# Chunk attention and FNet mixing: the token transform on even and odd tokens apart, in four 32-row parts

## The chip, the cores and the metric

The kernel runs on one core of one Trainium2 chip, in float32. Its time is the device time of one execution in microseconds. Nothing but the kernel's own launch is counted.

## The reference

```python
# q, k, v: [B=8, H=8, S=576, D=64]; attention inside chunks of 64 tokens
scores = (q_c @ k_c.T) / sqrt(D); attn = softmax(scores); x = attn @ v_c
x = x.transpose(0, 2, 1, 3).reshape(8, 576, 512)
mixed = real(fft(fft(x, axis=1), axis=2))     # over tokens, then over the 512 features
u = x + mixed
un = (u - mean(u)) / sqrt(var(u) + 1e-6)      # over the features
out = u + relu(un @ w_ch1[512, 2048]) @ w_ch2[2048, 512]
```

Two Fourier transforms of real data have symmetries. The sum of a row and its mirror image carries the cosine part, the difference the sine part, in tokens as in features, so that products of half the size do.

## The kernel before

**Tiles.** The 9 chunks of a batch are laid out as tiles of 128 rows: two LO tiles (chunks 2i and 2i+1), two HI tiles (the mirrored chunks from the end, 8-2i and 7-2i), and chunk 4, which two batches share as one tile of rests. For the mirroring the first token of each low chunk must stand one chunk further on: `shift(b)` (L477) moves six rows of 512 around, from tile to tile; it does so with six small DMAs, on GpSimd's queue for b = 1 and on SP's from b = 2. `shift_early` (L464) does the same for b = 0 with copies.

**Stages of a batch.** `attention(b)` computes a tile's transposes (L333), scores (`sc`, L384), softmax, and products with v (`att_V`, L432 to L460). `fold(b, i)` (L491) adds and subtracts a LO and a HI tile and their feature mirrors into `pm`: four quarters T = 0 to 3 of 128 columns, and one middle column; `i = NM = 2` is the tile of rests. GpSimd does this for b >= 2, VectorE for b = 1. `fourier(b)` (L644) is the token transform and then the feature transform. `product` (L652) multiplies the quarters of `pm` with the table `tk` of 289 = S/2 + 1 cosines or sines: eight matmuls of 128 rows x 289, four of 64 rows x 289 for the rests, and twelve one-column products for the middle columns, in four pieces of 73 or 70 each. ScalarE copies the results from PSUM into `zf` and `zr` (L678 to L688). `mixed(i)` (L700) multiplies them with the feature tables; `both` (L710, L711), `added` (L717) and `means` (L637 to L642) build u and the layer norm. Batch 0 has its own `fourier_early` (L745 and on).

**MLP.** The tiles go through the MLP in nine groups of 512 tokens: group g = 0 to 7 holds the LO and HI tiles of batch g, group 8 the four tiles of rests. Groups 0 and 1 use the weights as loaded, which VectorE and ScalarE round first (L285 to L322). For later groups seven products take the place of eight (`up_halves` with L1040, `down_halves` with L1089); their combined weights are computed while groups 0 and 1 run (`keep1`, `keep2`, stored to DRAM at L902 and L920) and fetched by SP as slabs (L926 to L932). A full MLP step is 16 passes of 128 x 256, 3.45 us of TensorE. GpSimd's largest share is L941, sums of pieces of `h` in which the MLP's products go on.

**Order.** Each engine runs its queue in program order. The main loop steps through `mlp(g)`; between two steps it advances the generator `side(b)` of the next batch as often as is needed to end at a given step (`ready_at`; the number of yields of a side stands in `sizes`). A side is `attention(b)`, then PAUSE = 3 empty steps, then `fourier(b)`. A step that returns true is "heavy": the rounding of the next weight piece is skipped beside it. Around Fourier in batch 2 the order on TensorE is: last product with v, 17.3 us of MLP, four token products, 3.5 us, the other twenty, 3.5 us, the first feature product. In odd batches from 3 it is 19.0 us of MLP, four products, 1.7, twenty, 6.9, feature products; in even ones from 4 it is 17.3, four, 3.5, twenty, 3.5.

**DMA.** SP issues nearly all transfers: q, k (L195), v (L218), the slabs and the stores. `store` (L871) writes a LO tile with one DMA, a HI tile with two, a tile of rests with four (of the last, half on ScalarE's queue). DMAs issued by SP and ScalarE take eight completion semaphores in turn, in program order over both, and a DMA waits with its issue for the one that had its semaphore before.

**Start.** `load_tables` (L224) loads the token tables with 8 DMAs; `turn_tables` (L248) turns them with five ScalarE copies into `tk` before batch 0's first products.

Of the kernel before, what the change touches and what calls it, by code (L numbers as in the profile page):

```python
# [8 lines left out]
FP32 = mybir.dt.float32  # L9
# [7 lines left out]
def kernel(  # L17
# [67 lines left out]
    tk = const.tile([128, NM + 1, 2, NQ], FP32, name="tk")  # L85
# [3 lines left out]
    so = const.tile([128, HQ], FP32, name="so")  # L89
    wa = const.tile([128, KD * DFF], FP32, name="wa")  # L90
# [71 lines left out]
    pms, sts = {}, {}  # L162
    start = one_p.tile([128, KF * 512], FP32, tag="big", name="start")
# [5 lines left out]
    v_ring = [const.tile([128, 2, NJ, DV], FP32, name=f"v{i}") for i in range(3)]  # L169
    more_v = one_p.tile([128, 4 * NL + 64], FP32, tag="zf", name="more_v")  # L170
# [4 lines left out]
    def load(n, which="qk"):  # L175
# [4 lines left out]
        for src, dst, nm, eng in ((q, qs, "q", nc.sync), (k, ks, "k", nc.scalar if n == 0 else nc.sync)):  # L180
            if nm not in which:
                continue
            if n < first[1]:
                i = 2 * n + (nm == "k")
                t = start[:, (4 + i) * DM:(5 + i) * DM].rearrange("p (j r d) -> p j (r d)", r=2, d=D)
            else:
                t = one_p.tile([128, NJ, 4 * D], FP32, tag=nm, name=nm)
# [36 lines left out]
    def load_tables():  # L224

        t = start[:, 0:(NM + 1) * 2 * NQ].rearrange("p (i r f) -> p i r f", i=NM + 1, r=2)
        for c in range(2 * NM):  # L230
            (i, r0), (j, p0) = divmod(c * CH, 128), divmod((NC - 1 - c) * CH, 128)
            nc.sync.dma_start(out=t[r0:r0 + CH, i], in_=seq_tab[p0:p0 + CH, j])
        for r0 in (0, CH):
            nc.sync.dma_start(out=t[r0:r0 + 1, NM], in_=seq_tab[0:1, 0])
            nc.sync.dma_start(out=t[r0 + 1:r0 + CH, NM], in_=seq_tab[1:CH, NM])
        for i in range(2):
            nc.sync.dma_start(out=first_rest[32 + 32 * i:33 + 32 * i, 0:DM], in_=dim_tab[0:1, 1 + 2 * i, :])
# [9 lines left out]

    def turn_tables():  # L248
        t = start[:, 0:(NM + 1) * 2 * NQ]
        a, b = tk.rearrange("p i r f -> p (i r) f"), t.rearrange("p (i f) -> p i f", f=NQ)  # L250
        for c in range(2 * NM):
            nc.scalar.copy(a[:, :, c * CH:(c + 1) * CH], b[:, :, (c + 1) * CH:c * CH:-1])
        nc.scalar.copy(a[:, :, NL:NL + 1], b[:, :, 0:1])
        nc.scalar.copy(a[:, :, NL + 1:NQ], b[:, :, NL + 1:NQ])
# [157 lines left out]
    def att_P(n):  # L412
        ex = es.pop(n)
        pt = turn(lambda j: ex[:, j].rearrange("p e k -> p (e k)"))
        t = one_p.tile([128, NJ, 128], FP32, tag="pT", name="pT")
        nc.scalar.copy(t, pt)
        pT[n] = t
# [45 lines left out]

    def shift_early(i):  # L464

        lows = [xt(at[LO, 0, j])[:, 0:DM] for j in range(NM)]
        rest, kept = xt(rests[0])[0:1, 0:DM], first_rest[0:1, 0:DM]
        if i == 0:
            nc.gpsimd.tensor_copy(kept, lows[1][0:1])
            nc.gpsimd.tensor_copy(lows[1][0:1], lows[1][CH:CH + 1])  # L470
            nc.gpsimd.tensor_copy(lows[1][CH:CH + 1], rest)
        else:
            nc.scalar.copy(rest, lows[0][0:1])
            nc.scalar.copy(lows[0][0:1], lows[0][CH:CH + 1])
            nc.scalar.copy(lows[0][CH:CH + 1], kept)

    def shift(b):  # L477

        lows = [xt(at[LO, b, i]) for i in range(NM)]
        r = b % 2 * CH  # L480
        rest = xt(rests[b // 2])[r:r + 1, 0:DM]
        eng = nc.gpsimd if b < 2 else nc.sync
        t = three_p.tile([128, XW], FP32, tag="y", name="first")
        for i in range(NM):
            eng.dma_start(out=t[2 * i:2 * i + 2, 0:DM], in_=lows[i][0:CH + 1:CH, 0:DM])
        eng.dma_start(out=t[2 * NM:2 * NM + 1, 0:DM], in_=rest)
        for i in range(NM):
            eng.dma_start(out=lows[i][0:CH + 1:CH, 0:DM], in_=t[2 * i + 1:2 * i + 3, 0:DM])
        eng.dma_start(out=rest, in_=t[0:1, 0:DM])

    def fold(b, i):  # L491
# [7 lines left out]
        if i < NM:  # L499
            pm = two_p.tile([128, DM + 1], FP32, tag="pm", name="pm")  # L500
# [5 lines left out]
        else:  # L506
            pm = two_p.tile([128, 2 * HQ + 1], FP32, tag="pm_rest", name="pm_rest")
# [10 lines left out]
        if i < NM:  # L518
# [3 lines left out]
            to = pm[:, 3 * HQ:DM + 1:HQ]  # L522
        else:
            for T, op in enumerate((ALU.add, ALU.subtract, ALU.subtract, ALU.add)):
                to = pm[T % 2 * CH:T % 2 * CH + CH, T // 2 * HQ:T // 2 * HQ + HQ]
                eng.tensor_tensor(out=to, in0=near[:, T // 2], in1=far[:, T // 2], op=op)
            to = pm[CH:, HQ:2 * HQ + 1:HQ]
        eng.tensor_copy(to, two[p, HM + 1 + HQ:HQ - 1:-HM - 1])
        pms[b, i] = pm

    def attention_early():
# [33 lines left out]
        turn_tables()  # L565
# [64 lines left out]
    zr = const.tile([128, 4, 2, CH], FP32, name="zr")  # L630
# [12 lines left out]

    def fourier(b):  # L644
        h = b % 2
        zf = one_p.tile([128, 4 * NL + 64], FP32, tag="zf", name="zf")
        zf = zf[:, 0:4 * NL].rearrange("p (t f) -> p t f", t=4)
        pm = [pms.pop((b, i)) for i in range(NM + 1)]

        def product(T, i, out_, lhsT, start, stop, cols=slice(0, NQ)):  # L650
            p = slice(0, 128) if i < NM else slice(T % 2 * CH, T % 2 * CH + CH)
            nc.tensor.matmul(  # L652
                out=out_, lhsT=lhsT[p], rhs=tk[p, i, T // 2 if T != 5 else 0, cols],
                start=start, stop=stop, skip_group_check=True,
            )


        z = [ps_t.tile([128, 512], FP32, tag="pt", name="z") for _ in range(2)]
        more = ps_a.tile([128, 2, 512], FP32, tag="att", name="more_z")
        z += [more[:, k] for k in range(2)]  # L660
        for T in range(4):
            for i in range(NM):
                product(T, i, z[T][:, 0:NQ], pm[i][:, T * HQ:(T + 1) * HQ], i == 0, False)
            if T == 1:
                yield
        for T in range(4):
            product(T, NM, z[T][:, 0:NQ], pm[NM][:, T // 2 * HQ:(T // 2 + 1) * HQ], False, True)

        mids = []
        for g, c0 in enumerate(range(0, NQ, NS)):  # L670
            c1 = min(c0 + NS, NQ)
            mids.append((c0, c1, z[2][32 * g:32 * g + 1, NQ:NQ + c1 - c0]))
        for i in range(NM + 1):
            for c0, c1, out_ in mids:
                one = pm[i][:, DM:DM + 1] if i < NM else pm[i][:, 2 * HQ:2 * HQ + 1]
                product(5, i, out_, one, i == 0, i == NM, slice(c0, c1))
        for T in range(4):
            nc.scalar.copy(zf[:, T, :], z[T][:, 0:NL])  # L678
            nc.scalar.copy(zr[:, T, h, 0:NQ - NL], z[T][:, NL:NQ])
            upper, mirrored = zr[:, T, h, NQ - NL:CH], z[T][:, NQ - 2:NL:-1]  # L680
            nc.scalar.activation(out=upper, in_=mirrored, func=ACTF.Copy, scale=1.0 if T < 2 else -1.0)
            for c0, c1, from_ in mids if T == 2 else ():
                n = max(0, min(c1, NL) - c0)
                if n > 0:
                    nc.scalar.copy(zf[0:1, T, c0:c0 + n], from_[:, 0:n])
                if c1 > NL:
                    nc.scalar.copy(zr[0:1, T, h, 0:NQ - NL], from_[:, n:])
                    nc.scalar.copy(zr[0:1, T, h, NQ - NL:CH], from_[:, NQ - 2 - c0:NL - c0:-1])  # L688
        yield
# [37 lines left out]
    def fourier_early():  # L727
# [3 lines left out]
        zf = one_p.tile([128, 4 * NL + 64], FP32, tag="zf", name="zf")  # L731
# [6 lines left out]
        mids = [(c0, min(c0 + NS, NQ)) for c0 in range(0, NQ, NS)]  # L738
        order = (1, 0, NM)
        for i in order:  # L740
            at_ = {"start": i == order[0], "stop": i == order[-1], "skip_group_check": True}
            for T in range(4):
                p = slice(0, 128) if i < NM else slice(T % 2 * CH, T % 2 * CH + CH)
                d0_ = T * HQ if i < NM else T // 2 * HQ
                nc.tensor.matmul(out=z[T][:, 0:NQ], lhsT=pm[i][p, d0_:d0_ + HQ], rhs=tk[p, i, T // 2], **at_)  # L745
            p, d0_ = (slice(0, 128), DM) if i < NM else (slice(CH, 128), 2 * HQ)
            for r, (c0, c1) in enumerate(mids):
                nc.tensor.matmul(
                    out=mid[32 * r:32 * r + 1, 0:c1 - c0], lhsT=pm[i][p, d0_:d0_ + 1], rhs=tk[p, i, 0, c0:c1], **at_
                )  # L750
        for T in range(4):
            if T % 2:
                nc.vector.tensor_copy(zf[:, T, :], z[T][:, 0:NL])
            else:
                nc.scalar.copy(zf[:, T, :], z[T][:, 0:NL])
        for r, (c0, c1) in enumerate(mids):
            n, from_ = min(c1, NL) - c0, mid[32 * r:32 * r + 1]
            if r % 2:
                nc.vector.tensor_copy(zf[0:1, 2, c0:c0 + n], from_[:, 0:n])
            else:  # L760
                nc.scalar.copy(zf[0:1, 2, c0:c0 + n], from_[:, 0:n])
        round_weight(1, put_off, "h")
        for T in range(4):
            nc.scalar.copy(zr[:, T, 0, 0:NQ - NL], z[T][:, NL:NQ])
            upper, mirrored = zr[:, T, 0, NQ - NL:CH], z[T][:, NQ - 2:NL:-1]
            nc.scalar.activation(out=upper, in_=mirrored, func=ACTF.Copy, scale=1.0 if T < 2 else -1.0)
            if T == 2:
                n = NL - c0
                nc.scalar.copy(zr[0:1, T, 0, 0:NQ - NL], from_[:, n:c1 - c0])
# [526 lines left out]
```

## Time and profile before

| what | us |
|---|---|
| three runs | 1089.86, 1090.85, 1091.65 |
| median | 1090.85 |
| profiled execution: span, first to last instruction | 1089.0 |
| TensorE busy (matmuls) | 1070.4 (98%) |
| VectorE, ScalarE, GpSimd busy | 577.2, 299.2, 280.3 |
| mean granted TensorE clock | 0.998 |

The profiled execution's own time is not given apart from its span; the span lies 1.85 us under the median of the runs, and 0.9 to 2.7 us under the single ones. What is worked out from the profile is therefore a difference to the span, and is set against the median with the same offset.

The page names a group by line, engine, operation, written and read tile, shape and count. "128*128 128x289" means a matmul with 128 rows and 128 weight columns whose moving operand is 128x289. Behind the bar stand the busy time in us and the mean of one in ns, then the engine's idle time just before and who ended it. The mean of one is longer than the distance between two, since matmuls are pipelined; where a rate matters, a stretch is measured. In the table of stretches each row is from:to, its length, TensorE's busy time (instructions), that of the weight loads, the clock, the share and rate of the DMA.

### The profile page before, as it was taken

Reading aid. Unit: us, or ns where it says so; the run is one execution under the profiler, and the core shown is the slowest. Engines: PE = TensorE matmul, PEld = TensorE weight load, DVE = VectorE, ACT = ScalarE, POOL = GpSimd, SP = SyncE. Lnnn points to the kernel's source line nnn. Section 1 sums busy time; section 2 is a strip of 40 time slices with the busy share of each in tenths; the row PEclk is TensorE's granted clock in tenths of the full one; section 3 lists DMA queues with packets and bytes.
Section 4 is the critical chain, followed back from the end, with each engine's and each line's share of the span. In section 5 each row is a group of like instructions: output and inputs, shape, how many; then the busy total and the mean of one; then the engine's idle time right before and its main releaser. Section 6 shows DMA issues by size and latency. Waiting matters only on the chain.

```text
span 1089.0 us, 18837 instructions
## 1 busy us (share of the span) xinstructions
PE 1070.4 (98%) x7018; PEld 848.7 (78%) x7018; DVE 577.2 (53%) x1258; ACT 299.2 (27%) x730; POOL 280.3 (26%) x403
## 2 busy tenths in 40 slices
PE   8999999999999999999999999999999999999998
PEld 6644454446888888888888888888888888888887
DVE  4899987314566355663556455735663534323411
ACT  4788453222113310322022212321133103101300
POOL 4301002444405140153114220514051401210140
PEclk9999999999999999999999999999999999999999
DMA  7777556679575637692668357854653455446232
GB/s 167 224 222 175 158 162 227 171 239 308 178 203 167 198 136 206 189 255 95 191 184 253 124 165 223 206 170 152 197 185 90 147 190 163 120 154 211 78 116 78
DMA packets 147970, 192.73 MB, mean 177 GB/s; under 512 B 66126, under 2 KB 104014, under 8 KB 140712
## 3 DMA queue, kind: packets, MB, share of 16 engines
q1 hardware_dynamic: 145620, 190.20, 58.4%
q8 instruction: 56, 0.92, 0.4%
q0 software_dynamic: 512, 0.68, 0.3%
q10 hardware_dynamic: 1748, 0.66, 0.2%
q14 instruction: 34, 0.28, 0.1%
HBM read 167.22 MB, written 24.12 MB: 176 GB/s over the span
## 4 chain that ended last, share of the span: by engine, by line
PE 89%; DVE 4%; ACT 2%; DMA 2%; SPq 2%; issue 1%; POOL 0%; DVEq 0%; ACTq 0%
PE pb L1089 20%; PE pa L1040 17%; PE pa L1089 15%; PE pb L1040 13%; PE up L973 4%; PE up L953 3%; PE pt L333 3%; PE dn L994 3%; PE mix L700 2%; PE sc L384 2%; PE more_z L652 2%; PE xp L432 2%; PE z L652 1%; PE idle L1167 1%; DMA xall<-in_moe_w_ch_dram 1%; SPq L195 1%
## 5 line engine op out<-in xcount | busy, mean ns | idle before, releaser
L1040 PE MATMUL pa<-unT,wa 128*128 128x256 f32 x672 | 159.5, 380 | 1.1 <-DVE wa L1048 1.1
L1040 PEld LDWEIGHTS pa<-unT,wa 128*128 128x128 f32 x672 | 126.5, 190 | 18.9 <-DVE wa L1048 1.5
L941 POOL TENSOR_TENSOR h<-h 128x256 f32<-128x256 f32 x64 | 55.7, 877 | 269.5 <-PE pb L1040 150.5
L1089 PE MATMUL pa<-wb,h 128*128 128x256 f32 x512 | 115.6, 380 | 0.0
L1089 PE MATMUL pb<-wb,h 128*128 128x256 f32 x512 | 114.9, 379 | 0.0
L1040 PE MATMUL pb<-wa 128*128 128x256 f32 x448 | 106.6, 381 | 0.0
L1089 PEld LDWEIGHTS pa<-wb,h 128*128 128x128 f32 x512 | 96.1, 190 | 13.5 <-issue 0.5
L1089 PEld LDWEIGHTS pb<-wb,h 128*128 128x128 f32 x512 | 96.3, 190 | 12.6
L1040 PEld LDWEIGHTS pb<-wa 128*128 128x128 f32 x448 | 84.2, 190 | 11.6 <-DVE h L1056 0.2
L994 PE MATMUL dn<-wb,h 128*128 128x512 f32 x128 | 58.4, 605 | 0.9 <-ACT h L964 0.9
L1046 DVE TENSOR_TENSOR wa<-pb,wa 128x256 f32<-128x256 f32 x56 | 23.5, 423 | 65.5 <-ACT wa L1045 65.5
L1089 PE MATMUL pb<-wb,yall 128*128 128x256 f32 x256 | 58.2, 381 | 0.0
L1089 PE MATMUL pa<-wb,yall 128*128 128x256 f32 x256 | 57.9, 380 | 0.0
L1089 PE MATMUL pb<-wb 128*128 128x256 f32 x256 | 57.7, 379 | 0.0
L973 PE MATMUL up<-unT,wa 128*128 128x512 f32 x128 | 56.8, 596 | 0.0
L1045 ACT COPY wa<-pa 128x256 f32<-128x256 f32 x56 | 20.8, 372 | 125.1 <-PE pa L1040 125.1
L1040 PE MATMUL pa<-wa 128*128 128x256 f32 x224 | 53.5, 382 | 0.0
L717 POOL TENSOR_TENSOR xall<-y,xall 128x513 f32<-128x513 f32 x14 | 21.3, 1518 | 125.3 <-DVE y L711 125.3
L1040 PE MATMUL pb<-unT,wa 128*128 128x256 f32 x224 | 52.9, 379 | 0.0
L1089 PEld LDWEIGHTS pa<-wb,yall 128*128 128x128 f32 x256 | 47.7, 190 | 6.4
L1089 PEld LDWEIGHTS pb<-wb,yall 128*128 128x128 f32 x256 | 47.7, 190 | 6.3
L1089 PEld LDWEIGHTS pb<-wb 128*128 128x128 f32 x256 | 47.6, 190 | 5.9
(250 smaller groups left out, 1685.0 us busy)
## 6 DMA issues: line engine op xcount, KB each, us to landing
wb<-s SPq DMA_DIRECT2D x56, 1024.0 KB
wa<-s SPq DMA_DIRECT2D x196, 256.0 KB
xall<-in_moe_w_ch_dram SPq DMA_DIRECT2D x22, 512.0 KB
q<-in_q_dram SPq DMA_DIRECT2D x96, 112.0 KB
k<-in_k_dram SPq DMA_DIRECT2D x96, 112.0 KB
v<-in_v_dram SPq DMA_DIRECT2D x124, 64.0 KB
yall<-in_moe_w_ch_dram SPq DMA_DIRECT2D x10, 512.0 KB
s<-wb SPq DMA_DIRECT2D x20, 256.0 KB
```

Source lines behind the costliest of these rows:

```text
L333: nc.tensor.transpose(pt[:, j, :], src(j), ident)
L384: nc.tensor.matmul(out=sc[t0:t0 + CH, e, j * CH:(j + 1) * CH], lhsT=a[r0:r0 + D, 2 * j + c, 0:CH], rhs=b[r0:r0 + D, 2 * j + c, 0:CH], star ...
L432: nc.tensor.matmul(out=xp[0][e][t0:t0 + CH, j * DV:(j + 1) * DV], lhsT=a[r0:r0 + CH, j, t0:t0 + CH], rhs=b[r0:r0 + CH, c, j, :], start=Tru ...
L652: nc.tensor.matmul(out=out_, lhsT=lhsT[p], rhs=tk[p, i, T // 2 if T != 5 else 0, cols], start=start, stop=stop, skip_group_check=True,)
L700: nc.tensor.matmul(out=mix[:, cols], lhsT=zt[:, T], rhs=tab, start=(T == 0), stop=(T == 3), skip_group_check=True,)
L941: nc.gpsimd.tensor_tensor(out=h1[:, m, hi], in0=h1[:, m, lo], in1=h1[:, m, hi], op=ALU.subtract)
L953: nc.tensor.matmul(out=up, lhsT=w1[:, kk, m * 128:(m + 1) * 128], rhs=unT[:, kk], start=(kk == 0), stop=(kk == KD - 1), skip_group_check=True,
L973: nc.tensor.matmul(out=up, lhsT=w1[:, kk, m * 128:(m + 1) * 128], rhs=unT[:, kk], start=(kk == 0), stop=(kk == KD - 1),)
L994: nc.tensor.matmul(out=dn, lhsT=h1[:, m, s * 128:(s + 1) * 128], rhs=w2[:, m, :], start=(m == 0), stop=(m == KF - 1),)
L1040: nc.tensor.matmul(out=dst, lhsT=w[:, kk, r], rhs=rhs[o][:, kk], start=(o in (0, 1) and kk == 0), stop=(kk == 1), skip_group_check=True,)
L1046: nc.vector.tensor_tensor(out=b, in0=pbs[r][:, 0], in1=a, op=ALU.add)
L1089: nc.tensor.matmul(out=dst, lhsT=lhs[:, m], rhs=w[:, m], start=(o in (0, 2) and m == 0), stop=(m == HF - 1), skip_group_check=True,)
```

## The change

The table `tk` holds only half the columns (NE = 145). Even and odd tokens stand apart: in each 64-row chunk of a tile the first 32 rows are the odd tokens and the last 32 the even ones (the copy of the attention's transposed weights, L416, permutes). The odd sum o and the even sum e of a token transform give two outputs at once, e + o and e - o. So the twelve products become five sets (`z_sets`) of eight matmuls of 32 rows x 145, each on one of the four 32-row parts of the array, with even and odd into PSUM banks of their own. Three sets (one of each tile and that of the rests) and the eight middle products of the tiles come first, then, a step later, the four middle products of the rests and the other set of each tile. New on ScalarE: `z_middle` (four one-row copies), `z_odd` (two copies 128x290), and the strided copies of `z_tile` and `z_rest` in place of L678 to L688. New on VectorE: `z_joined` (128x580, then two of 128x290).

Also changed: `shift` is six GpSimd copies of 1x512 in a row instead of DMAs, for all batches. `fold` has one more 128x1 operation, a product with a sign tile. `store` writes a LO tile with two DMAs, a HI tile with four (the even/odd second ones on ScalarE's queue), a tile of rests with six. `turn_tables` is gone; the token tables come in order with 10 DMAs into space behind wb, and one ScalarE copy makes `tk` at step t = 8. PAUSE is one less for all batches but 1, in which `fourier` has one step more; the steps with products and with the last copies of batch 1 are heavy. A few tiles are padded or stand elsewhere.

In the order on TensorE this gives for batch 2: last product with v, 13.8 us of MLP, three sets and eight middle products, 3.5 us, the rest, 6.9 us, the first feature product. Odd batches from 3: 12.1, 6.9, 8.6. Even batches from 4: 12.1, 5.2, 6.9. Batch 1: 10.4 us of MLP ahead of the first sets (13.8 before), then 6.9 and 3.5 (3.5 and 3.5 before).

```diff
-    tk = const.tile([128, NM + 1, 2, NQ], FP32, name="tk")
+    NE = NQ // 2 + 1
+    tk = const.tile([128, NM + 1, 2, NE], FP32, name="tk")
...
     def shift(b):
...
-        eng = nc.gpsimd if b < 2 else nc.sync
-        for i in range(NM):
-            eng.dma_start(out=t[2 * i:2 * i + 2, 0:DM], in_=lows[i][0:CH + 1:CH, 0:DM])
-        eng.dma_start(out=t[2 * NM:2 * NM + 1, 0:DM], in_=rest)
-        for i in range(NM):
-            eng.dma_start(out=lows[i][0:CH + 1:CH, 0:DM], in_=t[2 * i + 1:2 * i + 3, 0:DM])
-        eng.dma_start(out=rest, in_=t[0:1, 0:DM])
+        for to, from_ in ((kept, rest), (rest, a[r0]), (a[r0], a[r1]), (a[r1], c[r0]), (c[r0], c[r1]), (c[r1], kept)):
+            nc.gpsimd.tensor_copy(to, from_)
...
     def fold(b, i):
...
+        eng.tensor_tensor(out=pm[rows, m0 + 1:m0 + 2], in0=pm[rows, m0:m0 + 1], in1=sign[rows], op=ALU.mult)
...
+    def z_sets(z, pm, i, turn_, first=False):
+        for s in range(2):
+            for q_ in range(4):
+                k, r = (q_ // 2 + turn_) % 2, q_ % 2
+                T, p = 2 * k + s, slice(32 * q_, 32 * q_ + 32)
+                d0_ = T * HQ if i < NM else s * HQ
+                nc.tensor.matmul(
+                    out=z[r][k][:, s * NE:(s + 1) * NE], lhsT=pm[i][p, d0_:d0_ + HQ],
+                    rhs=tk[p, NM - 1 - i if i < NM else NM, k],
+                    start=first and s == 0, stop=False, skip_group_check=True,
+                )
+    def z_odd():
+        for k in range(2):
+            nc.scalar.copy(zs[0][:, 2 * k:2 * k + 2, 1], zs[2][k][:, 0:2 * NE].rearrange("p (t f) -> p t f", t=2))
+    def z_joined():
+        even = zs[1][:, :, 0:2 * NE].rearrange("p k (t f) -> p k t f", t=2)
+        z4 = zs[0].rearrange("p (k t) r f -> p k t r f", t=2)
+        nc.vector.tensor_tensor(out=z4[:, :, :, 0], in0=even, in1=z4[:, :, :, 1], op=ALU.add)
+        for k in range(2):
+            e, o = even[:, k], z4[:, k, :, 1]
+            a, b = (e, o) if k == 0 else (o, e)
+            nc.vector.tensor_tensor(out=o, in0=a, in1=b, op=ALU.subtract)
...
     def fourier(b):
...
+        z = z_space()
         for i in range(NM + 1):
+            z_sets(z, pm, i, 0, i == 0)
+        outs = [z[0][0][32 * g:32 * g + 1, 2 * NE:] for g in range(4)]
+        for i in range(NM):
+            mid_products(outs, pm, i)
+        nc.scalar.copy(middle[:, 0, 0:1], outs[0][:, 0:1])
+        yield b == 1
+        if b == 1:
+            yield
+        mid_products(outs, pm, NM)
+        for i in range(NM):
+            z_sets(z, pm, i, 1)
+        z_middle(outs)
+        z_odd()
+        if b == 1:
+            z_joined()
+        else:
+            yield
+            z_joined()
+        nc.scalar.copy(zs[0][0:1, 2], middle)
+        if h == 1:
+            z_rest(h)
+        for i in range(NM):
+            z_tile(zf, i)
+        if h == 0:
+            z_rest(h)
+        yield b == 1
...
     def store(n, o):
...
-            nc.sync.dma_start(out=to[:, ::-1], in_=o)
+            if kind(n) == LO:
+                to = out[b, t0 + 1:t0 + CH + 1, :][::-1].rearrange("(i r) d -> r i d", r=2)[::-1]
+                nc.sync.dma_start(out=to, in_=o[r0:r0 + CH])
...
-                nc.sync.dma_start(out=out[b, t0:t0 + CH, :], in_=o[r0:r0 + CH])
+                for r in range(2):
+                    eng = nc.scalar if r else nc.sync
+                    eng.dma_start(out=out[b, t0 + 1 - r:t0 + CH:2, :], in_=o[r0 + ODD * r:r0 + ODD * r + ODD])
...
-            for _ in range(PAUSE):
+            for _ in range(PAUSE if b == 1 else PAUSE - 1):
...
+                if t == 8:
+                    nc.scalar.copy(tk, early_tk[:, :, :, 0:NE])
```

## The prediction

> **What bounds the kernel now.** I read the head of the page first, then the shares of the chain that ended last, then the groups of instructions, then single stretches.
>
> ```profile
> PE 1070.4 (98%) x7018; PEld 848.7 (78%) x7018; DVE 577.2 (53%) x1258; ACT 299.2 (27%) x730; POOL 280.3 (26%) x403
> ...
> PE 89%; DVE 4%; ACT 2%; DMA 2%; SPq 2%; issue 1%; POOL 0%; DVEq 0%; ACTq 0%
> ```
>
> TensorE is busy for 1070.4 of 1089.0 us at a granted clock of 0.998, so about 19 us of idling is all that better order could win. The time must come out of the matmul rows. These are the rows that the change touches, of the groups with shapes apart, and below them the four stretches in which they run for batch 7, of that line alone:
>
> ```profile
> L652 PE MATMUL more_z<-tk,pm 128*128 128x289 f32 x56 | 14.8, 406 | 0.0
> L652 PE MATMUL z<-tk,pm 128*128 128x289 f32 x56 | 14.8, 406 | 0.0
> L652 PE MATMUL z<-tk,pm_rest 64*128 64x289 f32 x28 | 5.3, 455 | 0.0
> ```
>
> ```profile
> 827.90:829.85 1.95, 1.95 (x8) 1.32 (x7) 1.00 0.56 129
> 831.58:833.62 2.04, 2.04 (x9) 1.33 (x8) 1.00 0.24 86
> 833.62:834.79 1.17, 1.17 (x9) 0.69 (x8) 1.00 0.20 74
> 834.79:835.39 0.60, 0.60 (x26) 0.34 (x24) 1.00 0.00 0
> ```
>
> A float32 matmul shows as two records, its two passes. Eight records of 128x289 fill 1.95 us: 0.243 a pass. The third row is the rests, 64 rows each: eight passes in 1.17 us, 0.146 a pass, because two row tiles run side by side. The last row is the 24 passes of the one-column products. Together 5.76 us a batch, times seven batches 40.3 us. That is the sum the change works on.
>
> **What the Trainium skill says.** "TensorE: Matmul & The Clock Gate", Part 3: Packing small matmuls, says that matmuls on different 32-row groups run concurrently and that four with K=32, N=512 measured 3.07 times. "TensorEngine Tiling (Array Packing)", Key Properties, says that tiles load weights and multiply independently, and that a change of tiling mode drains the array. The trace shows pairs of 64-row tiles (0.146 us) and four 64x64 tiles in the scores L384 (starts 7 ns apart, a set every 0.058 us), and after the change of shape at the rests some 0.2 us lost (1.17 less 4 x 0.243); it shows no four 32-row tiles. "DMA: Bandwidth & Descriptors", Issuing engines are not separate DMA queues, says that issuing from a second engine saves issue time only; here ACT's queue moved 0.66 MB of 192.7, so no run yet shows that split.
>
> **The change part by part.**
>
> *Token products: removed and added.* The eight 128x289 matmuls and four 64-row ones go. In come five sets (two for each of the two tile pairs, one for the rests) of eight matmuls of 32 rows by 145 tokens. A set is two rounds of four row tiles in four PSUM banks, each of two passes. A pass of 145 at 0.243/289 a token is 0.122 us; 5 x 2 x 2 x 0.122 = 2.44 us. The twelve one-column products stay, 0.60. They now sit in two places, so the shape changes about four times where it changed twice; at 0.2 us each that is 0.85. Sum 3.9 against 5.76: **-1.86 us a batch, -13.0 us in all**. Weight loads of 0.19 us against passes of 0.122 are no bar by themselves: the eight 128-column passes of a mix (L700) take 1.10 us with loads of the same length. Ends: shape changes free, -18; loads half exposed, 0.16 a pass, -8.
>
> *Copies after them (ACT, DVE).* Even and odd sums must be joined: per batch ACT gets two 128x290 copies (the 256-wide row L678 is 0.38, so 0.4 each), four one-row copies at 0.21, and five strided copies to zf; DVE gets three tensor_tensors of 580, 290 and 290 elements, 1.65 us by L710's 0.42 per 255. From the end of the products to the mix that is 5.6 to 6.6 us. For odd b >= 3 8.6 us of MLP lies between, hidden. For even b it is 6.9 (two MLP steps of 3.45): hidden but thin, **+0.7** in all (0 to 3). PAUSE - 1 pays for this: the first set comes 3.45 to 6.9 us earlier after the attention. GpSimd's fold for b = 3 ended 7.2 us after the last attention product; the set now comes at 12.1. Slack 4.9, nothing lost.
>
> *Batch 1.* There weight rounding keeps ACT and DVE full, and the mix waited for these copies already:
>
> ```profile
> 150.84 0.72 ACT L306 ACTIVATE power<-power,top 128x512 uint32<-128x512 uint32 x1
> 151.47 0.35 ACT L678 COPY zf<-z 128x256 f32<-128x256 f32 x1
> ...
> 153.59 0.17 ACT L688 COPY zr<-more_z 1x31 f32<-1x31 f32 x1
> ```
>
> The rounding pieces end at 151.5, the copies follow, TensorE stands some 3 us until 155. After the change the chain of copies is some 2 us longer with the same 3.45 us of cover, but rounding is skipped at two steps. I take **+1** (-1 to +4). The rounding put off there ends two steps later, and DVE is the loaded engine until some 190 us.
>
> *Rows moved along.* Six SP DMAs (0.55 to 0.6 us of issue each) and their waits on each other go; six GpSimd copies of 1x512 come.
>
> ```profile
> 21.02 0.60 POOL L469 COPY first_rest<-xall 1x512 f32<-1x512 f32 x1 [13.18 <-DVE xall L449]
> 21.68 0.60 POOL L470 COPY xall<-xall 1x512 f32<-1x512 f32 x1
> ...
> 232.68 1.21 SPq L485 DMA_DIRECT2D first<-xall  x2
> 233.94 0.60 SPq L486 DMA_DIRECT2D first<-xall  x1
> 235.07 1.12 SPq L488 DMA_DIRECT2D xall<-first  x2
> 236.24 0.55 SPq L489 DMA_DIRECT2D xall<-first  x1
> ```
>
> SP is freed for 4.1 us a batch, GpSimd gets 6 x 0.66 = 4.0 us and one 128x1 operation (0.2) in each fold; at 26% busy it has room. What stands behind the copies on GpSimd's queue is the fold itself and the pieces of h (L941) that the MLP's next products read; for b = 2 the copies fall into a gap (216.6 to 221.6 us), and I cost them at nothing as long as such gaps stay; without one, 4 us in front of a fold that has 4.9 us of slack. The k loads behind the shift come earlier: **-0.5** (-1 to 0) where the chain showed them late (b = 3, 5).
>
> *Stores.* A LO tile goes out in two DMAs instead of one, a HI tile in four instead of two, the odd/even second ones on ACT's queue; a group of four gets 2 x 1 + 2 x 2 more, half on ACT. SP gets 2 more issues a group, some 1.2 us, less than the shift gave back. But DMAs take eight completion semaphores in turn over both queues: a DMA cannot be issued before the one eight places earlier has landed. ACT's HI stores of group 0 wait for DVE's output adds (189 to 192 us) and take places ahead of SP's stores of converted weights, which precede batch 2's v, q and k loads. Such waits are seen already:
>
> ```profile
> SPq L195 <- DMA wb<-s: 13.6, 7, 2.6
> ...
> SPq L488 <- DMA first<-xall: 9.6, 6, 3.5
> ```
>
> From 190 to 260 us SP issues without a pause, and the k load issued at 201.2 landed at 209.5, its scores ran at 210.8 with no wait; the next one waited 1.4 us. If the loads come 5 to 8 us later, TensorE stands. Then the fold of b = 2 ended at 258.0 before, and the set that needs it now comes 3.45 us earlier, while the fold no longer waits for the shift's landing (8.1 us at L504). I take **+4** for this stage (0 to +14).
>
> *Rest.* Tables are loaded in order, so the five ACT copies L252 to L254 before the first z go (29.7 to 31.8 us), but DVE's pm comes at 33.4: at most 0.3. One copy of tk at step 8, 1 us of ACT, hidden by a 3.45 us step. The tail has one more store on each queue: +0.3.
>
> Sum: -13.0 + 0.7 + 1 - 0.5 + 4 + 0.3 = **-7.5 us**. The profiled execution spans 1089.0, 1.85 under the median of the runs, 1090.85; with the same offset, 1081.5 + 1.85 = **1083.3**.
>
> **Rivals.**
> - *Gain in full.* The slot coupling finds the stores landed, the fold is in time: -13 + 2 = 1079 to 1080, and with cheap shape changes 1076. For it: SP is 4 us freer in each batch and POOL idles. Against: the stage at 200 to 260 us has no slack for k.
> - *Slower: the four row tiles do not run four at once.* If weight loads or passes of 32-row tiles go in pairs only, a set costs twice: 4.9 + 0.6 + 0.85 = 6.3 a batch, +4 us, and with the +5.5 of the stages 1100. It decides once a round of four passes takes over 0.21 us instead of 0.122 (20 rounds x 7 batches x 0.093 eats 13). For it: this trace shows at most two row tiles. Against: the scores run two row and two column tiles at once, and the skill's 3.07.
> - *The loads of batches 1 and 2 collapse.* Late stores on ACT's queue hold SP, q and k come 10 us late twice: 13 us or more of TensorE idle between 170 and 260, about 1091. No other place has so little slack.
> - *It doesn't do what it says.* If the tiles' weight loads are half exposed (0.16 a pass), -8 + 5.5 = 1088.
>
> **How the numbers follow.** The measurement can tell about 0.2%, 2.2 us, from no change. Chances: my sum (1080.5 to 1087) 0.45; the full gain (1075 to 1080.5) 0.27; loads half exposed or twice the stalls (1087 to 1090) 0.10; collapse around 1089 to 1097 0.10; row tiles in pairs, about 1100, 0.08. Faster by over 0.2% (under 1088.7) takes the first two and half the third: 0.77. Within 0.2%: 0.08. Slower: 0.15. The range 1075 to 1093 leaves out the pairs and the worst collapses.
>
> **What would show it.** Right: the new token products start four at a time within some 10 ns, a set of eight lasts near 0.5 us, the line sums to about 3.9 us a batch; TensorE busy near 1058; the shift absent from SP's queue; idle in 190 to 260 us larger by about 4. Wrong: sets of 1 us or more; scores of batch 2 waiting for kT by more than 8 us; mix waiting for zf in the even batches; fold's L504 late before the new set; or TensorE as idle as before with the time near 1078.

## The result, and the profile after

| kernel | median us | runs | ratio to before, 95% interval |
|---|---|---|---|
| before | 1090.55 (1086.94 to 1092.09) | 16 | |
| after | 1092.36 (1089.97 to 1096.78) | 16 | 1.0025 [1.0013, 1.0037] |

The kernel after is slower by 0.25%; a gain, to 1083.3, had been forecast. The profiled execution spans 1089.0 us as before, but it was the execution of 1090.81 us, one of the quicker ones. The head of its page and the shares of the chain that ended last:

```profile
PE 1056.8 (97%) x7410; PEld 840.4 (77%) x7410; DVE 590.6 (54%) x1287; ACT 309.5 (28%) x730; POOL 308.4 (28%) x459
...
PE 82%; DMA 5%; DVE 5%; SPq 3%; ACT 3%; issue 1%; POOL 0%; DVEq 0%; ACTq 0%; POOLq 0%
```

TensorE has 13.6 us less to do; 13.0 had been forecast. Yet its share of the chain fell from 89 to 82%, and DMA's rose from 2 to 5%: what the matmuls gave, waits took back. The gain itself came as planned. First the four stretches of batch 7 in which the token products run (TensorE alone; three sets, eight middle products, four middle products, two sets), then the first starts of a set:

```profile
823.58:825.27 1.69, 1.69 (x49) 1.00 0.58 139
825.27:825.63 0.36, 0.36 (x20) 1.00 0.98 381
832.74:832.97 0.23, 0.23 (x10) 1.00 0.94 365
832.97:834.17 1.20, 1.20 (x39) 1.00 0.44 137
```

```profile
823.58 0.39 PE L669 MATMUL z<-tk,pm 32*128 32x145 f32 x1
823.59 0.39 PE L669 MATMUL more_z<-tk,pm 32*128 32x145 f32 x1
823.59 0.39 PE L669 MATMUL z<-tk,pm 32*128 32x145 f32 x1
823.60 0.39 PE L669 MATMUL more_z<-tk,pm 32*128 32x145 f32 x1
823.81 0.28 PE L669 MATMUL z<-tk,pm 32*128 32x145 f32 x1
```

Four passes start within 20 ns; the first round after the change of shape takes 0.23 us, every further one of this set 0.12. A batch takes 3.48 us instead of 5.76: -2.28, or -16.0 if all seven batches run as batch 7 does, against -13.0 in the sum. TensorE's busy time fell by only 13.6, in part because some of its other work ran at half clock (below).

Where the rest went can be seen by comparing when the same MLP matmul starts in both kernels. By the time of the kernel before, the kernel after is 0.6 us behind at 102 us, 0.5 ahead at 178, 12.4 behind at 211 and 14.7 behind three and a half us later; from 260 us on it regains some 2 us with each batch and ends 0.5 behind. So one stage, 178 to 211 us, cost 13 us net. TensorE's longest waits name it:

```profile
PE sc L398 <- DVE rd L461: 10.1, 1, 10.1
PE pt L347 <- ACT un L942: 3.6, 3, 2.0
```

The scores of batch 2 wait 10.1 us. The chain that ended last shows what they waited for (start, length, what):

```profile
205.43 9.05 DMA out_dram<-o
...
215.35 6.14 DMA k<-in_k_dram
...
221.62 1.08 DVE kT L366
222.70 0.06 DVE rd L461 x2
222.76 1.13 PE sc L398 x32
```

The rd that ended their wait stands in VectorE's queue right behind the transposition of k, and that had waited for the landing of the k load, until 221.6. In the kernel before, the same transposition starts 12.1 us sooner:

```profile
209.55 1.12 DVE L352 STREAM_TRANSPOSE kT<-k 128x512 f32<-128x512 f32 x1 [6.93 <-DMA k<-in_k_dram]
```

These are SP's rows in the timeline of the kernel before (start, length of the issues, engine, line):

```profile
187.94 0.44 SPq L920 DMA_DIRECT2D s<-xall  x1
188.48 2.65 SPq L218 DMA_DIRECT2D v<-in_v_dram  x4
191.22 1.98 SPq L195 DMA_DIRECT2D q<-in_q_dram  x4
193.29 0.63 SPq L876 DMA_DIRECT2D out_dram<-o  x1
...
196.16 4.91 SPq L885 DMA_DIRECT2D out_dram<-o  x2
201.16 2.19 SPq L195 DMA_DIRECT2D k<-in_k_dram  x4
```

And the same stage in the timeline of the kernel after:

```profile
189.05 5.02 SPq L1021 DMA_DIRECT2D s<-yall  x3
...
195.75 2.64 SPq L226 DMA_DIRECT2D v<-in_v_dram  x4
198.48 1.99 SPq L203 DMA_DIRECT2D q<-in_q_dram  x4
200.51 0.43 SPq L1021 DMA_DIRECT2D s<-wb  x1
200.99 1.56 SPq L1021 DMA_DIRECT2D s<-xall  x3
202.59 1.45 SPq L1021 DMA_DIRECT2D s<-wb  x2
204.15 0.51 SPq L1021 DMA_DIRECT2D s<-xall  x1
204.76 1.21 SPq L977 DMA_DIRECT2D out_dram<-o  x2
...
209.43 2.52 SPq L986 DMA_DIRECT2D out_dram<-o  x2
212.04 3.74 SPq L203 DMA_DIRECT2D k<-in_k_dram  x4
```

The k load is issued from 212.0 on instead of 201.2. Seven stores of keep2 (L1021) that in the kernel before lay ahead of v now stand between q and k; and the three issues that took 5.02 us contain a wait of SP for stores of the output. ScalarE had issued these from 190.30 on, and SP's store needed a completion semaphore that one of them had taken (first line: SP's waits; second: ScalarE's timeline):

```profile
SPq L1021 <- DMA out_dram<-o: 3.8, 1, 3.8
190.30 2.56 ACTq L986 DMA_DIRECT2D out_dram<-o  x4
```

The load's own four issues contain one more such wait, of 2.1 us, for the store that the chain shows landing after 9.05 us; SP itself had issued that one. keep2's stores are late because its additions on VectorE are; its first one, in VectorE's timeline of the kernel before:

```profile
153.65 0.68 DVE L916 TENSOR_TENSOR yall<-wb 128x512 f32<-128x512 f32 x1
```

and in that of the kernel after:

```profile
171.39 0.68 DVE L1017 TENSOR_TENSOR yall<-wb 128x512 f32<-128x512 f32 x1
```

The program starts them only when the last weight piece is rounded, and the change puts rounding off at two steps of batch 1. The stall costs more than its length, for the granted clock (the third number from the end, in the stretches of the kernel after, all engines) falls in it and stays low for some microseconds after:

```profile
212.00:223.00 11.00, 0.90 (x41) 0.76 (x44) 1.30 (x4) 0.60 (x1) 0.00 (x0) 0.62 0.55 181
223.00:226.00 3.00, 3.00 (x35) 1.85 (x32) 2.14 (x4) 0.00 (x0) 2.28 (x2) 0.50 0.95 312
226.00:230.00 4.00, 4.00 (x7) 1.53 (x7) 0.00 (x0) 0.19 (x1) 3.88 (x5) 0.70 0.77 215
```

The means 0.62 and 0.70 come out if the clock was 1.00 until some 214.7 us, 0.50 from there to 228.4, and 1.00 again. The MLP falls a further 2.25 us behind there (12.44 to 14.69).

### The profile page after: what moved, and what is told of

Its sections match the earlier page's. It is cut to its first block, busy times and chain, and to the rows that moved or that the text cites. A ratio compares the mean times of both kernels' runs of the same rounds, so it can differ in the third digit from the quotient of the medians.

```text
span 1089.0 us, 19740 instructions
## 1 busy us (share of the span) xinstructions
PE 1056.8 (97%) x7410; PEld 840.4 (77%) x7410; DVE 590.6 (54%) x1287; ACT 309.5 (28%) x730; POOL 308.4 (28%) x459
## 4 chain that ended last, share of the span: by engine, by line
PE 82%; DMA 5%; DVE 5%; SPq 3%; ACT 3%; issue 1%; POOL 0%; DVEq 0%; ACTq 0%; POOLq 0%
PE pb L1190 20%; PE pa L1141 17%; PE pa L1190 15%; PE pb L1141 12%; PE up L1074 4%; PE dn L1095 3%; PE pt L347 2%; DMA wb<-s 2%; PE z L669 2%; PE mix L788 2%; PE xp L448 1%; SPq L216 1%; PE sc L398 1%; PE up L1054 1%; DMA out_dram<-o 1%
## 5 line engine op out<-in xcount | busy, mean ns | idle before, releaser
L505 POOL COPY xall<-xall 1x512 f32<-1x512 f32 x28 | 17.3, 620 | 149.7 <-DVE xall L465 120.4
L1074 PE MATMUL up<-unT,wa 128*128 128x512 f32 x128 | 59.1, 615 | 0.0
```

Of the source, the lines that this page charges most:

```text
L505: nc.gpsimd.tensor_copy(to, from_)
L1074: nc.tensor.matmul(out=up, lhsT=w1[:, kk, m * 128:(m + 1) * 128], rhs=unT[:, kk], start=(kk == 0), stop=(kk == KD - 1),)
```

## The experiments

Two causes are in question: **H**, rounding put off, and **A**, ScalarE's stores. All runs below are timed against the kernel before on the same chip. Its median moved between these comparisons (1090.13 to 1091.35), so a difference between runs of two comparisons is given by the ratios where that matters.

### Rounding not put off, in the kernel after

```diff
-        yield b == 1      # both places in fourier(b)
+        yield
```

> The kernel after, but the two Fourier steps of batch 1 that put off weight rounding (the two 'yield b == 1') are plain yields again, so that rounding and with it the weight combinations of keep2 come two MLP steps earlier. Theory H (put-off rounding delays keep2, whose seven stores then stand between q and k of batch 2 on SP): the k load of batch 2 starts at 201 to 205 us instead of 212, the scores' wait of 10.1 us falls under 4, and the time falls by 6 to 10 us, less up to 3 us that return as a wait of batch 1's first feature product. Theory A (ScalarE's stores hold the completion semaphores that SP's DMAs need): the k load stays after 209 us and the time falls by 2 us at most.

Measured: 1088.08 us, ratio 0.9973 [0.9963, 0.9984]; by the ratios 5.7 less than the kernel after (4.3 by the medians). The issue of the k load starts at 209.8, the scores wait 4.2 us. Batch 1's first feature product now waits 6.6 us where after waited 1.0. Time and wait are near H's figures, the start of k is A's: the late keep2 is one cause, and ScalarE's stores, which hold SP for 5.1 us in this run, are likely another.

### All stores on SP

```diff
-                    eng = nc.scalar if r else nc.sync
+                    eng = nc.sync
```

> The kernel after, but the second (even-token) stores of HI tiles are issued by SP as well, none by ScalarE. Theory A: the 3.8 us that SP waits at 189 us for out_dram and the 2.1 us ahead of the k load go, k starts 4 to 6 us earlier less 2.4 us for four more issues on SP; time 2 to 4 us less, in later batches the same. Theory H: k of batch 2 starts within 2 us of 212, time within 2 us of the kernel after.

Measured: 1087.66, ratio 0.9969 [0.9960, 0.9978]; by the ratios 6.1 less than after (4.7 by the medians). Yet the issue of k starts at 214.4 and the scores wait 9.9 us: what A expected of the load did not happen. SP has four more stores to issue, and with twelve stores over eight completion semaphores it waits 3.6 us for its own earlier stores to land before k's turn comes. By the starts of the same matmuls 2.4 us are won in the stage of batch 2 and 1.3 at batch 4, where TensorE's wait for VectorE's wa (L1149) is gone; 1.7 are lost ahead of 140 us, where the two kernels' order is the same: there this profile has 3.4 us at half clock (117.5 to 120.9), which the profile of after has not. These don't add up to the gain of the medians, and no single wait accounts for it.

### Both

> Both edits together: rounding not put off and all stores on SP. If H and A share the 13 us lost between 177 and 224 us, the scores wait of batch 2 is under 3 us and the time 1078 to 1082. If H alone is at work it equals the run without put-off rounding within 2 us. If neither, it stays at 1090 to 1093.

Measured: 1081.43, ratio 0.9916 [0.9900, 0.9932]. By the ratios that is less than after by 1.09% of the time of before, about the sum of the 0.52 and 0.56% of the two edits alone: the two causes add up. The scores' longest wait for a k load is 1.1 us, and what is left is above all the wait of batch 1 that put-off rounding had avoided:

```profile
PE mix L788 <- ACT zr L735: 6.8, 1, 6.8
PE dn L1095 <- ACT h L1065: 2.6, 1, 2.6
PE sc L398 <- DVE rd L461: 1.6, 2, 1.1
```

What counts is when k lands. The start of its issue misleads (us; k has landed when VectorE's transposition starts; TensorE is there when the scores' wait begins):

| run | issue of k starts | k landed | TensorE is there | scores wait |
|---|---|---|---|---|
| before | 201.2 | 209.6 | 210.8 | 0 |
| after | 212.0 | 221.6 | 212.7 | 10.1 |
| e1_no_heavy | 209.8 | 219.1 | 216.1 | 4.2 |
| e2_stores_sp | 214.4 | 220.8 | 212.0 | 9.9 |
| e3_both | 209.1 | 215.9 | 215.9 | 1.1 |

Between e1 and e3 only the stores differ: the issue starts at almost the same time, but k lands 3.3 us sooner, and the time falls by 6.7 us. 3.1 of these are the scores' wait; a stretch of 3.4 us at half clock behind it (220.3 to 223.7) and 1.8 us of waiting for wa (L1149) are gone as well. So A is a cause too. But e3 has no room to spare: k lands 6.3 us later than in the kernel before, and it is in time because batch 1's wait makes TensorE late as well.

### Rounding put off, in the kernel before

```diff
-            if T == 1:
-                yield
+                yield b == 1      # and likewise behind the copies
```

> The kernel before, with the two product steps of batch 1's Fourier marked heavy, so that rounding is put off there as in the kernel after; nothing else. Theory H: keep2's additions start some 15 us later than the 153.7 us of before, the k load of batch 2 starts 4 to 8 us later than 201.2, the scores wait 3 to 8 us and the time rises by 2 to 8 us although batch 1's first feature product waits up to 3 us less. Theory A: within 2 us of before, or faster by the 3 us of that wait.

Measured: 1100.85, ratio 1.0095 [1.0077, 1.0112]: 9.7 slower from this alone. keep2 starts some 17 us later than in before, the issue of the k load at 209.0 instead of 201.2, with seven stores of keep2 again between q and k, k lands at 218.1 instead of 209.6, and the scores wait:

```profile
PE sc L384 <- DVE rd L445: 9.2, 1, 9.2
```

That is more than the 2 to 8 expected. H is shown on the old products and the old stores; A has no part in it.

### The empty step of batch 1 moved behind the copies

```diff
-        if b == 1:
-            yield
         mid_products(outs, pm, NM)
...
         yield
+        if b == 1:
+            yield
```

> The kernel of e3_both, with the one empty step of batch 1's Fourier moved from between its two product steps to behind the last copies, so that 6.9 us of MLP instead of 3.45 cover the copies that the first feature product waits for (6.8 us in e3). Theory: that wait is only a matter of cover; it falls to 2 to 4 us, keep2 is not later than in e3, and the time falls by 3 to 4 us to 1077 to 1079. Rival: rounding fills ScalarE and VectorE whatever stands between, the copies move back with the products by as much, and the time stays within 1 us of e3.

Measured: 1078.96, ratio 0.9891 [0.9871, 0.9911], 2.5 less than e3. The wait for the copies is gone: the first feature product starts at 152.8 without one. Another of 4.0 us stands ahead of the third, at 162.7:

```profile
PE mix L788 <- DVE y L799: 4.0, 1, 4.0
```

VectorE rounds until 159.8 and makes three additions of keep2 before it takes the result of the first feature product out of the way. So the wait of e3 was a matter of cover, as the theory had it; that the new one lies within its 2 to 4 us is luck, for it is for something else.

### Group 0's stores on GpSimd

```diff
-                nc.sync.dma_start(out=to, in_=o[r0:r0 + CH])
+                (nc.gpsimd if n in groups[0] else nc.sync).dma_start(out=to, in_=o[r0:r0 + CH])
```

and likewise for HI tiles; on top of e5, and in e7 on top of e2.

> e5, and the twelve output stores of group 0 are issued by GpSimd instead of SP. Theory (these stores stand ahead of batch 2's k load on SP and hold completion semaphores): k is issued at 198 to 202 us, the scores of batch 2 do not wait, 1 to 3 us less than e5. Rival (no more is to be had there, or GpSimd's issues delay the shift and the pieces of h): equal to e5 within 1 us, or slower.

Measured: **1077.15**, ratio 0.9876 [0.9856, 0.9895]: 1.8 less than e5 and 13.0 less than before in the same comparison (1090.13), the best of all. k is issued from 195.8 on and lands at 207.0, the scores don't wait for it, and from 260 to 1075 us TensorE shows no wait for any engine. What the kernel before would gain if its own stores of group 0 went to GpSimd was not run.

> e2_stores_sp (rounding still put off, as in the kernel after), with group 0's stores issued by GpSimd. If SP's queue ahead of k is what turns the put-off rounding into a stall, the k load starts 6 to 10 us earlier than the 214.4 us of e2, the scores wait falls from 9.9 to under 4 us and the time is 1078 to 1083. If the late keep2 itself is the bar (its stores stay ahead of k), k starts after 208 us and the time stays over 1084.

Measured: 1081.42, ratio 0.9920 [0.9901, 0.9939]; by the ratios 5.3 less than e2 (6.2 by the medians). The issue of k starts at 208.8 instead of 214.4 and k lands at 213.5, the long wait of the scores is gone, and 4.2 us of waiting for the exponential (L424) stand in its place. The start of k fits the second expectation, the wait and the time the first. So put-off rounding hurts in good part through SP's queue; the wait that came shows that this is not all of it.

### The shift by DMA again

The six DMAs of before in place of GpSimd's copies, on top of e3.

> The kernel of e3_both with the rows moved along by six DMAs again (GpSimd's queue for batch 1, SP's from 2), as before. My prediction costs the shift at -0.5 us (up to -1): this run should then be 0 to 2 us slower than e3's 1081.4. Rival: the shift by DMA would now be late for the earlier first products (24 passes of fold's data, GpSimd waiting up to 8 us for the landing), 1 us or more in each batch, 5 to 10 us slower in all.

Measured: 1100.45, ratio 1.0089 [1.0063, 1.0115]: 19.0 slower than e3. Both expectations are missed. The comparison of starts with e3 puts 8.6 us at batch 1 and another 10 between batches 2 and 7, half of that at batch 4. Batch 1's part is one wait of VectorE:

```profile
DVE wb L322 <- DMA xall<-first: 9.3, 1, 9.3
```

Its next rounding piece stood behind the landing of the shift. Why it did so here and not in the kernel before, where the same DMAs are issued on GpSimd's queue at nearly the same time, is open.

### The shift by GpSimd alone, in the kernel before

> The kernel before, with nothing changed but the shift: six GpSimd copies of 1x512 instead of the six small DMAs, for all batches. The prediction costs this at -0.5 us (-1 to 0) in the order of the kernel before: 1089 to 1091 us. Rival, from the 19 us that the shift by DMA cost in e8: the DMAs' landing was on the path in the kernel before as well, and this run is 3 us or more faster than before.

Measured: 1088.87, ratio 0.9979 [0.9969, 0.9988]: 2.3 us by the ratio. Nearer the rival's 3 than the 0.5 of the prediction.

### The pause as long as before

```diff
-            for _ in range(PAUSE if b == 1 else PAUSE - 1):
+            for _ in range(PAUSE):
```

with one step more in `sizes`, on top of e6.

> The kernel of e6 with three empty steps after the attention in every batch again (and one step more in each side's count). The prediction costs the shorter pause at nothing, since the fold ends 4.9 us ahead of the new place of the first set. Theory: the time is within 2 us of e6's 1077.2. Rival: with one step more the sides' attention must start sooner, loads of q and k come under more pressure on SP, and the time rises by 3 us or more.

Measured: 1100.04, ratio 1.0082 [1.0065, 1.0098]: 22.9 slower than e6 (22.5 by the ratios). The rival, 3 us or more, came true, and far beyond its lower bound. TensorE's waits between 260 and 1075 us, where e6 has none:

```profile
PE pa L1141 <- DVE wa L1149: 12.4, 4, 4.5
PE pb L1141 <- DVE wa L1147: 1.9, 2, 1.2
```

These are 14.3 us; in them and behind them the profile has three stretches of 3.4 us at half clock. In batch 4 VectorE stood ahead of its transpositions of q and k, 4.5 and 4.8 us, for loads that had not landed; behind them in its queue were the results (L1149) that TensorE's next products wait for. Here the run changes two things at once, the place of the first products and the pace of the attention; the waits speak for the pace.

### One product step of two puts off rounding

e6 with `yield b == 1` at the first of the two places alone.

> The kernel of e6, in which the first product step of batch 1 alone puts off rounding. Batch 1's first feature product waited 4.0 us in e6; with one rounding piece less ahead of the copies on ScalarE and VectorE that wait falls to 1 to 2 us, while keep2 is about one step (4 to 8 us) later. If the k load now has room (group 0's stores are off SP), the time falls by 1 to 3 us to 1074 to 1076; if a later keep2 costs the stage as much as the wait, it stays at 1076 to 1080.

Measured: 1079.91, ratio 0.9896 [0.9879, 0.9913], 2.2 over e6 by the ratios (2.8 by the medians), with intervals that overlap. The wait was no longer one for the copies: in e6 as in e5 the third feature product waits for VectorE, and this did not fall (4.8 after 4.0); the waits for un (L942) rose from 1.6 to 2.9 us. Putting off one rounding gains nothing here.

## Why the prediction was wrong, point by point

- *Token products, -13.0.* Right in mechanism, a little low: -16.0 from the stretches. The term "changes of shape, 0.85" was too high: 1.69 + 1.20 less 20 rounds of 0.122 leaves 0.45 a batch. No pairs, no exposed weight loads: those two rivals are out. (With changes of shape free the working gives -19, not -18; and of the eight passes of L700 two have 256 columns. Neither is in the sum.)
- *Copies, +0.7.* Too pessimistic: in the kernel after no feature product of batches 2 to 7 waits; from 260 to 1075 us TensorE's only waits are 1.3 us for VectorE's wa (L1149).
- *Batch 1, +1.* The sign was wrong: TensorE's waits for these copies were 1.9 us (1.1 and 0.8; the prediction read some 3) and fell to 1.0. Putting rounding off did that: without it (e1) the wait is 6.6.
- *"The rounding put off there ends two steps later"* is **the step that failed**. It was written down and costed at nothing. Behind rounding stands keep2, behind keep2 its stores on SP, and behind these k of batch 2. e4 measures this alone: 9.7 us in the kernel before. In the kernel after it is worth some 6 us, net of what it saves at batch 1 (5.7 from after to e1, 6.2 from e2 to e3).
- *Stores, +4 (0 to +14).* The coupling by completion semaphores exists (3.8 us of SP's waiting in the profile after, 5.1 in e1), as the prediction said. ScalarE's stores cost some 6 us (6.1 from after to e2, 6.7 from e1 to e3), somewhat more than the middle value taken. (Of the six further stores of a group four go to ScalarE's queue, not half.) The stage cost 13 net, near the end of the bounds given, because both delays meet there, of which the sum held one. In time this is the rival "the loads of batches 1 and 2 collapse", about 1091, which had got 0.10; its cause, late stores on ScalarE's queue, is one of the two, and k came late once, not twice.
- *Shift, -0.5.* Mis-sized: -2.3 in the order of before (e9). In the order of after without rounding put off, the DMAs cost 19 (e8), but 8.6 of these come from a wait that stays unexplained.
- *PAUSE - 1, nothing.* Judged only by GpSimd's slack ahead of the first set. The waits of e10 say that it also sets the pace at which q and k are asked for; 22.9 us hang on it and the step that goes with it.
- *Clock.* Not thought of: a stall of 10 us cost 2.25 more in the matmuls behind it.

A time as in the rival of the full gain, 1076 to 1080, was there to be had: e6 reached 1077.15, by order and choice of queues alone.

## What to carry to other kernels

Follow a step that is put off through every queue behind it until something waits for the last of them: here one flag on rounding passed through VectorE and SP to a load that TensorE needed 60 us later. Where two delays meet in a queue that has no slack, add them: here neither hid behind the other. Judge a load by when it lands, not by when its issue starts. And judge a pause between stages by the loads whose pace it sets, not only by the work that it waits for.

## What of the hardware was not expected

Four 32-row matmuls of 145 columns did start within 20 ns and ran a round in 0.12 us, with weight loads of 0.184 us hidden beside them; the Trainium skill ("TensorE: Matmul & The Clock Gate", Part 3: Packing small matmuls) has 3.07 times at 512 columns. Here 80 passes ran in 2.89 us with the changes of shape; one after the other they would take 9.8 us, an estimate from the 0.243 us of a 289-column pass in the kernel before. That is 3.4 times.

TensorE's granted clock fell to 0.50 at some 214.7 us, only 2 us after the matmuls had stopped (212.65), and was back at full speed at 228.4, some 5.6 us after work resumed (222.75).
